# Attention, Fourier mixing and an MLP in one kernel: the first pass of the second product summed over two chunks in PSUM

## The chip, the cores and the metric

The kernel runs on one core of a Trainium2 chip. The metric is the time of one execution on the device in microseconds (us), the median over the runs. Five engines work side by side, each on its own queue in program order: TensorE (PE, with weight loads as PEld), VectorE (DVE), ScalarE (ACT), GpSimd (POOL) and SyncE (SP), which issues the transfers. Matmuls write into PSUM, eight banks per core; everything else lies in SBUF.

## The reference

Inputs are q, k and v of shape (4, 12, 448, 64) and two weight matrices in 64-bit floats, 768 x 3072 and 3072 x 768.

```python
scores = where(causal_mask, -1e9, q @ k.T / sqrt(64))
x = softmax(scores) @ v                      # to (4, 448, 768)
mixed = real(fft(fft(x, axis=1), axis=2))    # along rows, then along columns
u = x + mixed
un = (u - mean(u)) / sqrt(var(u) + 1e-6)
out = u + maximum(un @ w_ch1, 0) @ w_ch2
```

## The kernel before

All products are done with operands split in a high and a low part in the format fp32r: a product is three matmuls, high x high, high x low and low x high, summed in PSUM. Names ending in h and l are these parts.

The program is not written in the order in which it runs. Each step is declared with `add` (an engine or a choice of engines, a cost, a priority, what it reads and writes); `Plan.order` (line 101) then picks step by step the one that can start first by these costs, with the priority to break ties, and chooses between VectorE, ScalarE and GpSimd where a step may run on several. So a changed cost, priority or buffer count can move instructions on all engines, in stages that the change does not name too. The constants at the top (lines 30 to 51) set priorities and buffers.

The stages are: attention (`attend`) for 24 pairs of heads; `fold` and `dft`, the Fourier transform as products with cosine and sine tables, then the normalization; then the MLP. The MLP goes over the 1792 rows in two passes ("groups" g = 0 and 1, two batches or 896 rows each) and in each pass over 12 chunks of 256 hidden columns (`items`, line 708). For a chunk j:

- `weights` (line 723) loads a half (128 x 768) of w1 or w2 as 64-bit numbers, 32-bit words in pairs, and makes 32-bit floats of them with integer and float operations on the words: two on ScalarE (lines 742 and 746), three on VectorE (lines 752, 758 and 762). In the first pass there are 48 such halves. The buffers are w (raw) and w32 (result), two each. For w2 a ScalarE cast makes the high part w2h (line 775) and GpSimd the low part w2l (line 779); there are four buffers of each. Results are also stored to DRAM for the second pass. `halves` splits w1 into its parts (w1, with sums in ws, lines 811 and 824).
- `f1` (line 987) makes the first product into PSUM banks "h". Up to chunk 4 of the first pass, four blocks of the result take eight block products of nine matmuls each (448 columns). From chunk C_FAST = 5 on, and in the whole second pass, `fast` holds: the four blocks are made by seven block products, with sums and differences of the operands (names t1 to t4, s1 to s4). In these, a bank is gone on with after its content has been copied out ("c", line 335 on ScalarE) or added to a copy (line 1051 on VectorE). `finish` writes relu(h) as hh (ScalarE, line 1009) and hl (VectorE, line 1015). There are two buffers of hh and of hl. `kept` chunks leave their w1 parts in DRAM for the second pass.
- `f2` (line 1159) makes the second product. In the first pass, for each of seven blocks of 128 rows and two halves of the 768 columns, six matmuls of 384 columns (two halves of the chunk, three parts) go to a bank "o2" (line 1219), and VectorE adds it to the accumulator "acc" in SBUF (line 1168). That is 14 additions per chunk. In the second pass (`twice`) it is done in seven products again (line 1180).

Around it, `prep`, `mixed` and `refill` make the operands u and t of a pass. The loop at the end (from line 1251) declares for each j the weights ahead of time, then f1 of chunk j + 1 and f2 of chunk j: the first product of the next chunk runs between the matmuls of the second product of this one.

## Time and profile before

| | before |
|---|---|
| median of 3 runs | 944.24 us (944.07 to 949.7) |
| span of the profiled execution | 942.7 us (its own time isn't listed) |
| TensorE busy | 903.4 us, 96% of the span, 5636 matmuls |
| VectorE busy | 796.9 us, 85%, 1330 instructions |
| GpSimd busy | 627.6 us, 67%, 648 |
| ScalarE busy | 545.3 us, 58%, 1300 |
| moved by DMA | 165.84 MB, mean 176 GB/s |

The span runs from the first to the last instruction of the profiled execution; the times of the runs hold a little more. Shares of busy time are means over stages with different limits, so the sections below read them by stage. Matmuls overlap, and the end of one is modelled, so a matmul's duration is about twice the distance at which the next one starts; the distance between starts is what a matmul costs. In the timeline a row gives its start, its duration, and in brackets how long the engine idled before it and for what.

### The profile page before, as it was taken

The numbers are of one execution on the slowest core, as the hardware profiler recorded it, in microseconds if no ns is written. First come the engines' busy times: TensorE is split into PE (matmuls) and PEld (weight loads), VectorE is DVE, ScalarE is ACT, GpSimd is POOL, SyncE is SP. The second block draws the span as 40 slices with busy tenths as digits, with TensorE's granted clock in tenths as the row PEclk, the third lists the DMA queues.
The fourth block names the chain that finished last, engine by engine and source line by source line (L and its number), as shares of the span: only waits on it lengthen the run. The fifth ranks groups of instructions, "written<-read, shape, count | busy, mean of one in ns | idle before, by whom it ended". The sixth has DMA issues, their size and how long they took to land.

```text
span 942.7 us, 16159 instructions
## 1 busy us (share of the span) xinstructions
PE 903.4 (96%) x5636; PEld 805.8 (85%) x5636; DVE 796.9 (85%) x1330; ACT 545.3 (58%) x1300; POOL 627.6 (67%) x648
## 2 busy tenths in 40 slices
PE   7999999999799999999999988999999999999998
PEld 4667668777688999988989887998999999999998
DVE  6889999898897887999998999997788676666668
ACT  6999798988644444545454456645454453444442
POOL 4798698884642222443543337799999898887886
PEclk9999999999899999999999999999999999999999
DMA  7624624615569556758777668665123444444403
GB/s 274 220 88 170 183 77 138 164 45 180 149 210 345 171 208 224 245 196 292 277 275 256 214 217 295 210 217 174 48 68 118 129 139 136 141 145 136 149 1 117
DMA packets 67537, 165.84 MB, mean 176 GB/s; under 512 B 18976, under 2 KB 31904, under 8 KB 67360
## 3 DMA queue, kind: packets, MB, share of 16 engines
q1 hardware_dynamic: 67456, 164.82, 52.8%
q8 instruction: 44, 0.72, 0.3%
q14 instruction: 37, 0.30, 0.1%
HBM read 112.89 MB, written 54.74 MB: 178 GB/s over the span
## 4 chain that ended last, share of the span: by engine, by line
PE 60%; DVE 21%; POOL 6%; issue 6%; ACT 6%; DMA 1%; SPq 0%; POOLq 0%; DVEq 0%; ACTq 0%
PE h L978 22%; PE o L1180 16%; PE o L1219 8%; PE x L531 4%; PE pt L505 3%; PE sc L457 3%; DVE acc L1168 3%; DVE w L762 3%; DVE w L752 2%; ACT p L473 2%; DVE w L811 1%; DVE w L758 1%; DVE mn L469 1%; DVE ws L824 1%; DVE hl L1015 1%
## 5 line engine op out<-in xcount | busy, mean ns | idle before, releaser
L1168 DVE TENSOR_TENSOR acc<-o,acc 128x384 f32<-128x384 f32 x444 | 236.8, 552 | 79.9 <-PE o L1180 56.3
L1219 PE MATMUL o<-w2l,hh 128*128 128x384 f32 x336 | 113.6, 338 | 1.4 <-POOL w2l L779 1.3
L1219 PE MATMUL o<-w2h,hh 128*128 128x384 f32 x336 | 113.3, 337 | 1.6 <-DVE acc L1168 1.6
L1219 PE MATMUL o<-w2h,hl 128*128 128x384 f32 x336 | 113.1, 337 | 0.0
L779 POOL TENSOR_TENSOR w2l<-w,w2h 128x768 fp32r<-128x768 f32 x24 | 49.7, 2071 | 78.6 <-ACT w2h L775 71.6
L494 POOL TENSOR_TENSOR p<-p,ri 128x128 f32<-128x128 f32 (+3 forms) x113 | 79.1, 729 | 22.0 <-DVE ri L485 18.1
L811 POOL TENSOR_TENSOR w<-w,w 128x384 fp32r<-128x384 f32 x33 | 39.7, 1203 | 60.1 <-ACT w L335 59.1
L978 PE MATMUL h<-u11h,w 128*128 128x448 f32 x174 | 64.8, 380 | 3.4 <-ACT u11h L335 3.0
L1219 PEld LDWEIGHTS o<-w2l,hh 128*128 128x128 f32 x336 | 63.1, 188 | 4.4 <-POOL w2l L779 2.6
L1219 PEld LDWEIGHTS o<-w2h,hh 128*128 128x128 f32 x336 | 63.2, 188 | 4.2 <-DVE acc L1168 2.3
L978 PE MATMUL h<-u22h,w 128*128 128x448 f32 x174 | 63.2, 371 | 3.2 <-DVE c L1051 3.2
L1180 PE MATMUL o<-w2h,hh 128*128 128x384 f32 x288 | 65.1, 339 | 0.3 <-DVE acc L1168 0.3
L978 PE MATMUL h<-u12h,w 128*128 128x448 f32 x174 | 64.1, 370 | 0.0
L1219 PEld LDWEIGHTS o<-w2h,hl 128*128 128x128 f32 x336 | 63.2, 188 | 0.0
L978 PE MATMUL h<-u21h,w 128*128 128x448 f32 x174 | 63.0, 367 | 0.0
L1180 PE MATMUL o<-w2l,hl 128*128 128x384 f32 x288 | 62.4, 338 | 0.4 <-DVE acc L1168 0.4
L505 PE MATMUL pt<-cst,p 128*128 128x128 f32 (+1 forms) x384 | 56.9, 281 | 2.6 <-ACT p L492 1.9
L505 PEld LDWEIGHTS pt<-cst,p 128*128 128x128 f32 (+1 forms) x384 | 41.4, 139 | 16.8 <-issue 5.7
L335 ACT COPY c<-h 128x448 f32<-128x448 f32 x57 | 30.1, 529 | 44.1 <-PE h L978 40.2
L867 POOL TENSOR_TENSOR w2h<-w,w2h 128x384 fp32r<-128x384 f32 x43 | 45.8, 1065 | 14.6 <-ACT w2h L335 14.6
L473 ACT ACTIVATE p<-sc,mn 128x448 f32<-128x448 f32 (+3 forms) x96 | 50.4, 525 | 7.6 <-DVE mn L469 6.7
L1180 PEld LDWEIGHTS o<-w2h,hh 128*128 128x128 f32 x288 | 52.1, 188 | 2.6 <-DVE acc L1168 0.6
(212 smaller groups left out, 2999.7 us busy)
## 6 DMA issues: line engine op xcount, KB each, us to landing
w<-in_w_dram SPq DMA_DIRECT2D x48, 768.0 KB, 4.9
wp<-w SPq DMA_DIRECT2D x49, 384.0 KB, 3.5
w<-wp SPq DMA_DIRECT2D x49, 384.0 KB, 3.1
wf<-w SPq DMA_DIRECT2D x34, 384.0 KB, 2.9
w<-wf SPq DMA_DIRECT2D x17, 768.0 KB, 4.3
raw<-in_qk_dram SPq DMA_DIRECT2D x23, 480.0 KB, 3.8
us<-und SPq DMA_DIRECT2D x45, 224.0 KB, 4.2
v<-in_vv_dram SPq DMA_DIRECT2D x24, 256.0 KB, 2.9
```

Of the source, the lines that this page charges most:

```text
L335: nc.scalar.copy(out=out, in_=in_)
L473: nc.scalar.activation(out=T[pb][:, PO[rr]:PO[rr] + n], in_=T[ps][:, c0:c0 + n], func=ACTF.Exp, scale=-1.0, bias=T[mn][:, rr:rr + 1], accu ...
L494: nc.gpsimd.tensor_tensor(out=x, in0=x, in1=z.to_broadcast([128, KE[r]]), op=ALU.mult)
L505: nc.tensor.transpose(T[ps][0:m, 128 * k:128 * k + 128], T[pb][:, PO[r] + 128 * c:PO[r] + 128 * c + m], T["cst", 0][:, 0:128])
L531: nc.tensor.matmul(out=T[xps][64 * h:64 * h + 64, q0:q0 + w], lhsT=T[v][0:kk, c, h * D:(h + 1) * D], rhs=T[src][0:kk, s0 + h * sd:s0 + h * ...
L779: nc.gpsimd.tensor_tensor(out=T[wl], in0=T[w32].bitcast(F32), in1=T[wh], op=ALU.subtract)
L811: (nc.gpsimd if eng == "G" else nc.vector).tensor_tensor(out=T[z][:, 1], in0=src(), in1=T[z][:, 0], op=ALU.subtract)
L867: (nc.gpsimd if eng == "G" else nc.vector).tensor_tensor(out=T[z][:, 384:768], in0=src(), in1=T[z][:, 0:384], op=ALU.subtract)
L978: nc.tensor.matmul(out=T[ps][:, 0:S], lhsT=a[:, t], rhs=x[:, t], start=start and k == 0, stop=stop and k == 8, skip_group_check=True)
L1168: nc.vector.tensor_tensor(out=x, in0=T[ps][:, 0:384], in1=x, op=ALU.add)
L1180: nc.tensor.matmul(out=T[ps][:, 0:384], lhsT=hpart(j, h, a)[:, k * 128:k * 128 + 128], rhs=T[z][:, 384 * b:384 * b + 384], start=start and ...
L1219: nc.tensor.matmul(out=T[ps][:, 0:384], lhsT=T[a][:, m, k * 128:(k + 1) * 128], rhs=w[:, sl], start=(m == 0 and z == 0), stop=(m == 1 and ...
```

## The change

In the first pass the second product is made for two chunks at once: f2 runs for odd j only and sums the four halves of chunks j - 1 and j, twelve matmuls into a bank, before VectorE adds it to the accumulator. The accumulators are loaded at chunk 1 instead of 0. The declarations of a pair change with it: f1 of both chunks of the next pair follows f2 of this one (`f1_at`, `ahead`), the weights are declared in the order of their priorities (`jobs`), and a set of constants gives the places.

In the conversion of weights a third ScalarE operation puts the sign into the top byte of the low word, and the VectorE operation that took it from the high word (line 752) is dropped; the scale goes from the minimum on VectorE (line 758) to ScalarE's absolute value.

The raw and converted weights get three and four buffers instead of two and two, w1 eight instead of seven; the room is taken from the scratch for DMA descriptors, set to 1024 bytes. C_FAST goes from 5 to 4, so chunk 4 of the first pass is done in seven products too. SLOW and LATER, with which the planner chooses between engines, and the places MIX_LEAD and FILL_LEAD change.

```diff
-N_RAW, N_V, N_QK, N_PT, N_W, N_W32, N_PA = 2, 2, 3, 2, 2, 2, 2
+N_RAW, N_V, N_QK, N_PT, N_W, N_W32, N_PA = 2, 2, 3, 2, 3, 4, 2
-W_LEAD, F2_LAG = 809, 561
+W_LEAD, F2_LAG = 362, 453
+PAIR_F1, PAIR_GAP, PAIR_LEAD, F2_PAIR, PAIR_STEP, PAIR_W = 967, 652, 1010, 100, 67, 140
-N_W1, N_C, N_WS, C_FAST, C_MIX = 7, 3, 3, 5, 7
-MIX_LEAD, FILL_LEAD = -94, 417
-LATER = dict(S=-1500, V=-248, G=-847)
+N_W1, N_C, N_WS, C_FAST, C_MIX, N_W2 = 8, 3, 3, 4, 8, 4
+MIX_LEAD, FILL_LEAD = -372, 141
+LATER = dict(S=-1500, V=-599, G=-787)
-SLOW, BIAS = 1.5, dict(S=-300, V=-100, G=-500)
+SLOW, BIAS = 1.639, dict(S=-300, V=-100, G=-500)
...
-            nc.scalar.activation(out=T[w32].bitcast(F32), in_=T[w][:, :, 1].bitcast(F32), func=ACTF.Abs)
+            nc.scalar.activation(out=T[w32].bitcast(F32), in_=T[w][:, :, 1].bitcast(F32), func=ACTF.Abs, scale=W_SCALE)
...
-            x = T[w][:, :, 1]
-            nc.vector.scalar_tensor_tensor(
-                out=x, in0=x, scalar=0x80000000, in1=T[w][:, :, 0], op0=ALU.bitwise_and, op1=ALU.bitwise_or)
+            nc.scalar.activation(
+                out=T[w].bitcast(I8)[:, :, 3], in_=T[w][:, :, 1].bitcast(F32), func=ACTF.Prelu, scale=SIGN_SCALE, alpha=SIGN_ALPHA)
...
-            nc.vector.tensor_scalar(out=x, in0=x, scalar1=W_HIGH, scalar2=W_SCALE, op0=ALU.min, op1=ALU.mult)
+            nc.vector.tensor_scalar(out=x, in0=x, scalar1=W_TOP, scalar2=None, op0=ALU.min)
...
-                out=T[w32], in0=T[w32], scalar=3, in1=T[w][:, :, 1], op0=ALU.logical_shift_left, op1=ALU.bitwise_or)
+                out=T[w32], in0=T[w32], scalar=3, in1=T[w][:, :, 0], op0=ALU.logical_shift_left, op1=ALU.bitwise_or)
...
-        hh, hl = ("hh", j), ("hl", j)
+        js = (j - 1, j)
...
-                    for m in range(2):
-                        wh, wl = T["w2h", (j, m)], T["w2l", (j, m)]
+                    for q, (y, m) in enumerate((y, m) for y in js for m in range(2)):
+                        hh, hl, wh, wl = T["hh", y], T["hl", y], T["w2h", (y, m)], T["w2l", (y, m)]
...
-                                start=(m == 0 and z == 0), stop=(m == 1 and z == 2))
+                                start=(q == 0 and z == 0), stop=(q == 3 and z == 2))
...
-            f1(j + 1, when(j))
-        f2(j, when(j) + F2_LAG, 1000 / 14)
+        elif j % 2:
+            f2(j, when(j - 1) + F2_PAIR, PAIR_STEP)
+            for k in ((j + 1, j + 2) if j + 1 < NCH else (j + 1,)):
+                ahead(k)
...
-    nc = _bacc.Bacc("TRN2", target_bir_lowering=False, num_devices=1)
+    nc = _bacc.Bacc("TRN2", target_bir_lowering=False, num_devices=1, dynamic_dma_scratch_size=1024)
```

What the planner makes of it stands in two places. The first is TensorE's queue in the middle of the second product of the first pass, with matmuls as out<-moving operand, weights; o2 is a bank of the second product, h one of the first. Before:

```order
L1219 MATMUL o2_6333<-w2h_6153,hh_5885 128x384
L1219 MATMUL o2_6333<-w2l_6164,hh_5885 128x384
L1219 MATMUL o2_6333<-w2h_6153,hl_5897 128x384
L978 MATMUL h_6322<-u21h_3954,w1_6284 128x448
L978 MATMUL h_6322<-u21l_3978,w1_6284 128x448
L978 MATMUL h_6322<-u21h_3954,w1_6284 128x448
L1219 MATMUL o2_6351<-w2h_6123,hh_5885 128x384
L1219 MATMUL o2_6351<-w2l_6128,hh_5885 128x384
L1219 MATMUL o2_6351<-w2h_6123,hl_5897 128x384
L1219 MATMUL o2_6351<-w2h_6153,hh_5885 128x384
L1219 MATMUL o2_6351<-w2l_6164,hh_5885 128x384
L1219 MATMUL o2_6351<-w2h_6153,hl_5897 128x384
```

And now, one bank:

```order
L1221 MATMUL o2_6913<-w2h_6497,hh_6526 128x384
L1221 MATMUL o2_6913<-w2l_6508,hh_6526 128x384
L1221 MATMUL o2_6913<-w2h_6497,hl_6538 128x384
L1221 MATMUL o2_6913<-w2h_6503,hh_6526 128x384
L1221 MATMUL o2_6913<-w2l_6521,hh_6526 128x384
L1221 MATMUL o2_6913<-w2h_6503,hl_6538 128x384
L1221 MATMUL o2_6913<-w2h_6570,hh_6682 128x384
L1221 MATMUL o2_6913<-w2l_6582,hh_6682 128x384
L1221 MATMUL o2_6913<-w2h_6570,hl_6692 128x384
L1221 MATMUL o2_6913<-w2h_6646,hh_6682 128x384
L1221 MATMUL o2_6913<-w2l_6657,hh_6682 128x384
L1221 MATMUL o2_6913<-w2h_6646,hl_6692 128x384
```

Before, six matmuls made a bank and first products stood between the banks. Now twelve make one, from two hidden tiles and four halves of w2, and the 14 banks of a pair follow one another, with at most three first-product matmuls among them: 168 matmuls, then a block of 105 to 150 first-product matmuls, and so on through the pass.

The second place is TensorE's queue inside the first product of a chunk done in seven products, where bank h changes from the operand t3 to t4. Before:

```order
L978 MATMUL h_6280<-t3l_4512,w1_6358 128x448
L978 MATMUL h_6280<-t3h_4508,w1_6358 128x448 x2
L978 MATMUL h_6280<-t3l_4512,w1_6358 128x448
L978 MATMUL h_6280<-t3h_4508,w1_6358 128x448
L978 MATMUL h_6280<-t4h_5402,w1_6361 128x448
L978 MATMUL h_6280<-t4l_5413,w1_6361 128x448
L978 MATMUL h_6280<-t4h_5402,w1_6361 128x448 x2
L978 MATMUL h_6280<-t4l_5413,w1_6361 128x448
```

And now:

```order
L980 MATMUL h_7079<-t3h_4462,w1_7091 128x448 x2
L980 MATMUL h_7079<-t3l_4475,w1_7091 128x448
L980 MATMUL h_7079<-t3h_4462,w1_7091 128x448
L980 MATMUL h_7249<-u11h_7159,w1_7208 128x448
L980 MATMUL h_7249<-u11l_7240,w1_7208 128x448
L980 MATMUL h_7249<-u11h_7159,w1_7208 128x448
L980 MATMUL h_7256<-u21h_7173,w1_7212 128x448
L980 MATMUL h_7256<-u21l_7188,w1_7212 128x448
L980 MATMUL h_7256<-u21h_7173,w1_7212 128x448
L980 MATMUL h_7079<-t4h_5114,w1_7133 128x448
L980 MATMUL h_7079<-t4l_5138,w1_7133 128x448
L980 MATMUL h_7079<-t4h_5114,w1_7133 128x448
```

Before, t4 followed t3 in the same bank with nothing between them. Now six matmuls into two other banks, of the next chunk, stand there.

## Rows read from the trace of the kernel before

**Rows 1.** The page's head: the span.

```profile
span 942.7 us, 16159 instructions
```

**Rows 2.** Busy time by stretch: stretch, its length, PE, PEld, DVE, ACT, POOL, PEclk, DMA.

```profile
0.00:241.50 241.50, 227.44 (x2042) 165.41 (x2042) 208.64 (x432) 209.98 (x650) 183.95 (x240) 1.00 0.49 155
241.50:292.60 51.10, 46.48 (x273) 42.80 (x274) 46.81 (x69) 25.30 (x47) 26.68 (x26) 0.93 0.67 204
292.60:645.30 352.70, 336.62 (x1766) 317.20 (x1765) 318.52 (x457) 177.67 (x297) 161.50 (x118) 1.00 0.70 242
645.30:939.20 293.90, 292.83 (x1559) 280.40 (x1557) 222.35 (x373) 132.37 (x308) 255.46 (x267) 1.00 0.34 109
...
300.00:380.00 80.00, 80.00 (x428) 76.53 (x427) 64.58 (x104) 38.39 (x58) 18.46 (x13) 1.00 0.61 213
380.00:640.00 260.00, 244.91 (x1286) 229.87 (x1285) 245.45 (x344) 133.30 (x230) 136.39 (x99) 1.00 0.71 246
```

**Rows 3.** TensorE's timeline, 331 to 342 us: start, duration, what.

```profile
331.47 0.34 PE L1219 MATMUL o<-w2h,hh 128*128 128x384 f32 x1
...
332.52 0.36 PE L978 MATMUL h<-u11h,w 128*128 128x448 f32 x1
...
333.13 0.34 PE L1219 MATMUL o<-w2h,hh 128*128 128x384 f32 x1
...
336.45 0.37 PE L978 MATMUL h<-u12h,w 128*128 128x448 f32 x1
...
339.55 0.34 PE L1219 MATMUL o<-w2h,hh 128*128 128x384 f32 x1
...
341.64 0.37 PE L978 MATMUL h<-u22h,w 128*128 128x448 f32 x1
```

**Rows 4.** TensorE's timeline where it idled; in brackets the idling and its releaser.

```profile
294.71 0.45 PE L1219 MATMUL o<-w2l,hh 128*128 128x384 f32 x1 [0.99 <-POOL w2l L779]
...
552.90 0.47 PE L978 MATMUL h<-t4h,w 128*128 128x448 f32 x1 [0.62 <-ACT c L335]
...
556.75 0.47 PE L978 MATMUL h<-u22h,w 128*128 128x448 f32 x1 [1.75 <-DVE c L1051]
...
585.80 0.48 PE L978 MATMUL h<-t4h,w 128*128 128x448 f32 x1 [2.78 <-ACT c L335]
...
639.84 0.74 PE L978 MATMUL h<-t2h,w 128*128 128x448 f32 x1 [2.33 <-ACT c L335]
640.38 0.58 PE L978 MATMUL h<-t2l,w 128*128 128x448 f32 x1
640.75 0.58 PE L978 MATMUL h<-t2h,w 128*128 128x448 f32 x1
```

**Rows 5.** Groups by form: busy us, mean ns of one, idle us before them.

```profile
L1168 DVE TENSOR_TENSOR acc<-o,acc 128x384 f32<-128x384 f32 x444 | 236.8, 552 | 79.9 <-PE o L1180 56.3 <-PE o L1219 20.6
...
L762 DVE SCALAR_TENSOR_TENSOR w<-w,w 128x768 uint32<-128x768 uint32 x48 | 54.1, 1128 | 0.2
...
L752 DVE SCALAR_TENSOR_TENSOR w<-w 128x768 uint32<-128x768 uint32 x48 | 52.0, 1083 | 1.4 <-ACT w L742 1.0 <-ACT w L746 0.2
...
L746 ACT ACTIVATE w<-w 128x768 uint32<-128x768 uint8 x48 | 43.8, 913 | 12.9 <-DMA w<-in_w_dram 10.4 <-DVE t2l L905 2.5
...
L758 DVE TENSOR_SCALAR w<-w 128x768 f32<-128x768 f32 x48 | 34.4, 719 | 0.6 <-ACT w L742 0.6
...
L335 ACT COPY c<-h 128x448 f32<-128x448 f32 x57 | 30.1, 529 | 44.1 <-PE h L978 40.2 <-POOL us L1118 3.6
```

**Rows 6.** One line each: durations in ns, min/median/max, first and last start.

```profile
L752 DVE SCALAR_TENSOR_TENSOR w<-w x48: 909/953/2260, 119.8 to 610.9; 128x768 uint32<-128x768 uint32 x48
...
L758 DVE TENSOR_SCALAR w<-w x48: 507/551/1514, 132.7 to 610.4; 128x768 f32<-128x768 f32 x48
...
L762 DVE SCALAR_TENSOR_TENSOR w<-w,w x48: 941/949/2586, 137.7 to 612.2; 128x768 uint32<-128x768 uint32 x48
...
L775 ACT CAST w2h<-w x24: 820/834/840, 290.1 to 613.7; 128x768 fp32r<-128x768 f32 x24
...
L779 POOL TENSOR_TENSOR w2l<-w,w2h x24: 1837/1858/3950, 291.0 to 615.6; 128x768 fp32r<-128x768 f32 x24
```

More of the change, by code (lines that the diff above doesn't have):

```diff
@@ L14 @@
 U8 = mybir.dt.uint8
+I8 = mybir.dt.int8
 ACTF = mybir.ActivationFunctionType
@@ L1249, in w1s, with f1_at, go, ahead @@
         halves(j, p0 + 10)
+    def f1_at(j):
+        if items[j][0]:
+            return when(j - 1), 1.0
+        if j < 2:
+            return when(-1) + PAIR_GAP * j, 0.5
+        return when(j - j % 2 - 2) + PAIR_F1 + PAIR_GAP * (j % 2), 0.5
     prep(0, when(-1) - 300)
[L1252 removed]
+    jobs = []
     for j in range(J):
[L1254 to L1257 removed]
+        p = f1_at(j)[0] - W_LEAD if j else when(-1) - 300
+        jobs.append((p, len(jobs), lambda j=j, p=p: w1s(j, p)))
         if twice(j):
[L1259 to L1270 removed]
+            def go(j=j, p=when(j) - W_LEAD + 750):
+                weights(j, "2", 1, p)
+                quarters(j, p)
+            jobs.append((when(j) - W_LEAD + 750, len(jobs), go))
+        else:
+            for half in range(2):
+                p = when(j - j % 2) + F2_PAIR - PAIR_LEAD + PAIR_W * (2 * (j % 2) + half)
+                jobs.append((p, len(jobs), lambda j=j, p=p, half=half: weights(j, "2", half, p)))
+    for _, _, go in sorted(jobs, key=lambda x: x[:2]):
+        go()
+    def ahead(j):
+        if items[j] == (0, C_FAST):
+            mixed(0, f1_at(j)[0] - MIX_LEAD, False)
+        if items[j] == (0, C_MIX):
+            mixed(1, f1_at(j)[0] + 500, True)
+        if items[j] == (1, 0):
+            refill(1, f1_at(j)[0] - FILL_LEAD)
+        f1(j, *f1_at(j))
+    ahead(0)
+    ahead(1)
+    for j in range(J):
+        if twice(j):
+            if j + 1 < J:
+                ahead(j + 1)
+            f2(j, when(j) + F2_LAG, 1000 / 14)
+        elif j % 2:
+            f2(j, when(j - 1) + F2_PAIR, PAIR_STEP)
+            for k in ((j + 1, j + 2) if j + 1 < NCH else (j + 1,)):
+                ahead(k)
     seq = plan.order()
```

41 lines of the change are left out of this document (14 added, 27 removed).

## The prediction

> **What bounds the kernel now.** I began with the span and then cut it into stages by the busy time of each engine [rows 1, 2]. The reader is to see four stages: attention and Fourier transform (0 to 241.5 us), a crossover (241.5 to 292.6), the first pass of the MLP (292.6 to 645.3) and the second pass (645.3 to 939.2). TensorE is busy for 91% or more of each (227.44 of 241.5, 46.48 of 51.1), so it sets the end, and what a change elsewhere is worth is only the time in which TensorE stands still for it. That time is not spread evenly. The second pass has 292.83 us busy of 293.90; the first pass has 336.62 of 352.70, so 16.1 us of visible idling. Inside the first pass it sits in one part: from 300 to 380 us TensorE is busy for 80.00 of 80.00 us, with VectorE at 64.58 (81%) and GpSimd at 18.46 (23%); from 380 to 640 us it is 244.91 of 260, with VectorE at 245.45 (94%) and GpSimd at 136.39 (52%) [rows 2].
>
> A busy TensorE still hides small gaps, so I also counted. In the timeline six matmuls of the second product (384 columns) start within 1.05 us, 0.175 each, and three of the first (448 columns) within 0.61 us, 0.2033 each [rows 3]. The first pass holds 12 x 84 = 1008 of the former, and by the order of the program 756 of the latter (1764 together; the window counts 1766). That is 176.4 + 153.7 = 330.1 us of work in 352.7: 22.6 us are lost there, and this is what the change can win.
>
> Where they are lost the waits say [rows 4]. From chunk 5 on the first product is done in seven products instead of eight, which share a bank: before "t4" may go on in it, ScalarE must have copied out what "t3" left (a copy of 0.529 us [rows 5]). TensorE idles there for 0.62 us at the least and 2.78 at the most (five such rows before 640 us, 6.0 us), and 1.75 at "u22", which waits for VectorE's addition (three rows, 3.2 us). VectorE is late since its queue is full, and what fills it can be read off its groups: the additions to the accumulators (444 x 0.552 us) and three operations per half of weights in the conversion, 48 x 1.128, 48 x 1.083, 48 x 0.719 [rows 5].
>
> **The change part by part.** *Sum of two chunks in PSUM.* In the first pass 168 additions become 84: 84 x 0.552 = 46.4 us less on VectorE. The matmuls stay.
>
> *Conversion.* VectorE loses 48 x 1.083 = 52.0 us. ScalarE gains 48 instructions; no row has that function with an 8-bit result, the nearest (an 8-bit source, same 768 elements) takes 0.913, so 43.8 us. Bounds: 0.529 (the shortest row of that size class) and twice 0.913; I take 0.913. ScalarE is busy 177.67 of 352.7 us in the first pass, so there is room on average; its in-order queue is a rival below. The order has one table load in either program, so the new function brings none.
>
> *What moves.* VectorE goes from 1328 to 1247 instructions, not by 132 but by 81: 51 come over or are new, most of them from GpSimd (628 to 600). At the 0.719 to 1.128 of its two-operand and long rows I price them at 0.88, 45 us. VectorE in the first pass: 318.5 - 46.4 - 42 x 1.083 (six halves are converted before it) + 45 = 272 us of some 338, 80%: the load at which TensorE lost nothing visible between 300 and 380 us.
>
> *The order on TensorE.* Before, nothing stands between "t3" and "t4"; now six matmuls of other banks do, 1.2 us, more than the 0.529 us copy, and "t4" and "u22" come in threes by turns. So most of the 9.2 us in those eight rows should go.
>
> *What is late next.* A sum over two chunks needs both hidden tiles and four halves of w2, and there are just two hidden and four w2 buffers: nothing of the next pair can be written until the last matmul of this pair has read. Before, the first such start waited 0.99 us for GpSimd's w2l [rows 4]. I allow 1 us for each of six pairs, and 0.4 us for each of eight seven-product chunks: 9 us lost in place of 22.6, so 13.6 gained. Bounds: 0 lost (300 to 380 us) and 22.6.
>
> *One more chunk in seven products* (chunk 4): nine matmuls less, 9 x 0.2033 = 1.8 us. Its extra additions fall on VectorE (three, 1.8 us) under the cover above.
>
> *Long blocks.* First-product matmuls alone start 0.2067 us apart (15 in 3.10), not 0.2033; second-product ones alone 0.1742 (12 in 2.09), not 0.175 [rows 3]. 663 x 0.0034 - 1008 x 0.0008 = 1.4 us lost.
>
> *Attention and crossover.* Two more halves are converted during attention and the constants shift a few operations; ScalarE is busy 209.98 of 241.5 there. Two halves are six ScalarE and four VectorE instructions, some 9 us beside TensorE's 227: from 4 us lost to 3 gained, I take 0. In the crossover VectorE is busy for 46.81 of 51.1 us [rows 2] and loses an operation per half: 1 us gained, bounds 0 and 3. The smaller scratch for DMA descriptors only frees room: in the order every transfer stands in SyncE's queue and none in GpSimd's; taken at 0 (bounds -1 and +1).
>
> **Sum** against the profiled execution: 942.7 - 13.6 - 1.8 + 1.4 - 1 = 927.7 us of span. That execution's own time is not listed; the median 944.24 stands 1.5 us above its span, so 929 us.
>
> One rule speaks to the size of this. VectorE's conversion steps have medians of 0.953, 0.551 and 0.949 us but reach 2.26, 1.51 and 2.59, and GpSimd's w2l goes from 1.84 to 3.95 [rows 6]. The Trainium skill, page "SBUF — State Buffer", section "SBUF: two separate sides", says VectorE and GpSimd take their common port pair as an exclusive lock, so that the second waits for the whole instruction of the first. The long maxima agree with that. By it a first pass with less on GpSimd gets its medians back, 42 x (0.168 + 0.179) = 14.6 us less on VectorE, 76% busy, the load of the second pass, and I would put the loss at 5 us and the time at 925. I stay with the means.
>
> **Rivals.** *Nothing gained (0.16).* The 51 instructions fill VectorE again and the copies stay late: 22.6 us lost as before, and only 1.8 - 1.4 gained: 944. For it: the program was balanced by moving work over. Against: the six matmuls between "t3" and "t4" don't depend on VectorE's load.
>
> *ScalarE becomes the late one (0.10).* Each half now puts three instructions of 0.91 us on ScalarE, and a copy that TensorE waits for stands behind one of them. Eight chunks with three copies each, at half an instruction, 24 x 0.46 = 11 us: 940. For it: the row with 2.78 us. Against: ScalarE had half its time free.
>
> *The pair starts late, slower than before (0.11).* Between two pairs' sums TensorE has only the first products of two chunks, 105, 117, 138, 147 and 150 matmuls by the order, 21.3 to 30.5 us. In that time four halves of w2 must go through ScalarE, VectorE twice, ScalarE and GpSimd. Wholly in series at these rows' medians a half takes 0.913 + 0.551 + 0.949 + 0.834 + 1.858 = 5.1 us, four 20.4; at the maxima 9.8 and 39.2. If it takes 33 us, the five blocks are overrun by 11.7 + 9.2 + 4.9 + 3.1 + 2.5 = 31 us, less the 5 allowed: 955, and after such gaps the clock falls too (after 2.33 us of idling matmuls started 0.37 us apart instead of 0.2033 [rows 4], the level of 1.2 GHz): 957. It decides from about 32 us on. Against: two of the four halves are converted before the block starts.
>
> *Everything hidden (0.03):* no loss in the first pass, 920.
>
> *The forecast (0.60):* 929, its own range 920 to 938.
>
> **How the numbers follow.** A measurement of this kernel can tell about 1% from no change. Faster by more (under 934.8): the forecast but for its upper tail, and the hidden case, 0.64. Within 1%: nothing gained, ScalarE late, a little of the forecast, 0.25. Slower (over 953.7): 0.11. The range goes from 917 (all hidden and 3 us at the crossover) to 946, which takes in "nothing gained" with 2 us lost in attention; outside are the late pair and a little below.
>
> **What would show it.** Right: the addition to the accumulators at 360 instructions; VectorE at 78 to 83% of the first pass; TensorE's visible idling there at 5 to 8 us instead of 16, "t4" no longer a row with over 1 us; first pass 337 to 341 us long, the second within 2 us of 293.9, the start of the first second-product matmul within 3 us of 292.6. Wrong: waits of TensorE for w2l over 2 us at the start of a pair (then the late pair), waits for c copies behind weight conversions (then ScalarE), VectorE above 90% (then nothing gained), or a shift before 292.6 us, which I put at 0 or 1.

## The result and the profile after

The changed kernel takes 958.32 us (median of 4 runs, 955.77 to 960.02) against 944.79 us before: a ratio of 1.0126, interval 1.0094 to 1.0158. It is slower by 1.3%, where 1.6% faster was forecast, and lies above the range. The profiled execution took 957.12 us with a span of 955.3 us, 12.6 us over the span of before [rows 1].

A row product is a block product of the MLP's first product, into the banks "h". Busy time by stretch, cut where the first row product starts, where the first second product starts (the first pass) and where the last second product of that pass ends, answers to [rows 2]: stretch, length, PE, PEld, DVE, ACT, POOL with instruction counts, granted clock, DMA share, GB/s.

```profile
0.00:248.70 248.70, 233.76 (x2043) 170.11 (x2043) 213.06 (x448) 218.15 (x651) 180.93 (x238) 0.98 0.50 160
248.70:301.45 52.75, 48.82 (x275) 43.56 (x274) 42.75 (x66) 31.22 (x52) 23.18 (x25) 0.88 0.69 225
301.45:641.20 339.75, 322.51 (x1674) 302.53 (x1673) 244.63 (x368) 228.06 (x302) 95.33 (x61) 0.98 0.69 242
641.20:951.80 310.60, 309.28 (x1641) 296.23 (x1639) 219.64 (x374) 141.50 (x327) 273.23 (x288) 1.00 0.34 114
```

VectorE did what was forecast: in the first pass it is busy 244.63 of 339.75 us, 72%, where it was 90%. TensorE got nothing for it. With the distances between matmuls of the prediction (1008 x 0.175, and 663 row matmuls by the timeline x 0.2033) the first pass holds 311.2 us of work in 339.5: 28.3 us are lost, where 22.6 were. I use this "loss" for every run below. The 12.6 us are then:

| | before | after | |
|---|---|---|---|
| start of the first row product | 241.5 | 248.7 | +7.2 |
| crossover | 51.2 | 52.8 | +1.5 |
| loss of the first pass | 22.6 | 28.3 | +5.7 |
| nine row matmuls fewer (chunk 4) | | | -1.8 |

The first pass is 13 us shorter and the second 17 us longer: 84 row matmuls (17.1 us) moved from one to the other, as they now stand behind the last second product of the first pass. The second pass loses no more than before.

What TensorE waits for, from the view of waits (operation, releaser: us in total, times, longest). Before:

```profile
PE h L978 <- ACT c L335: 9.3, 7, 2.8
PE at L695 <- DVE un L685: 3.8, 4, 2.0
PE h L978 <- DVE c L1051: 3.2, 3, 1.7
PE h L978 <- ACT u11h L335: 3.0, 1, 3.0
PE h L978 <- DVE u11l L905: 2.6, 1, 2.6
...
PE h L978 <- DVE w L811: 0.4, 1, 0.4
```

After:

```profile
PE at L698 <- DVE un L688: 8.0, 5, 4.2
PE h L980 <- ACT w L338: 3.7, 3, 1.5
PE h L980 <- ACT c L338: 3.4, 7, 1.2
PE h L980 <- DVE w L813: 3.1, 4, 1.7
PE h L980 <- DVE u21l L907: 2.5, 1, 2.5
PE h L980 <- DVE c L1053: 2.0, 3, 1.3
PE o L1221 <- POOL w2l L781: 1.7, 2, 1.3
```

The wait for the copies "c" fell from 9.3 to 3.4 us, as forecast. In its place stand waits for parts of w1 (3.7 for ScalarE's high parts, 3.1 for VectorE's low parts, 0.4 before). Around the first row product the waits only change their name: "un" has 8.0 us for 3.8 (4.18 of it right before that product), and the parts of "u" have 2.7 (2.49 and 0.23) for 5.6. In the timeline, beside [rows 4]:

```profile
247.66 1.35 PE L698 MATMUL at<-cst,un 112*128 112x112 f32 x6 [4.18 <-DVE un L688]
...
255.99 0.74 PE L980 MATMUL h<-u21l,w 128*128 128x448 f32 x1 [2.49 <-DVE u21l L907]
...
419.56 0.47 PE L980 MATMUL h<-u11h,w 128*128 128x448 f32 x1 [1.46 <-ACT w L338]
...
528.30 0.48 PE L980 MATMUL h<-t4h,w 128*128 128x448 f32 x1 [0.43 <-ACT c L338]
537.98 0.47 PE L980 MATMUL h<-u11h,w 128*128 128x448 f32 x1 [1.41 <-ACT w L338]
...
602.53 0.74 PE L980 MATMUL h<-u21h,w 128*128 128x448 f32 x1 [0.77 <-DVE w L813]
```

"t4" no longer waits over 0.5 us; a new chunk's "u11" and "u21", which need a part of w1 just made, do. Neither belongs to the sums over pairs alone. Two runs below, e6 and e14, sum over pairs with the old conversion, and in the first pass they wait for w1 parts 0 and 0.7 us and for the copies again 8.3 and 9.7 (e6, then e14):

```profile
PE h L981 <- ACT c L338: 8.3, 5, 4.0
...
PE h L981 <- ACT c L338: 9.7, 10, 2.2
```

Groups, beside [rows 5]:

```profile
L1170 DVE TENSOR_TENSOR acc<-o,acc 128x384 f32<-128x384 f32 x360 | 195.7, 555 | 111.2 <-PE o L1182 58.0 <-PE o L1221 51.8
...
L754 ACT ACTIVATE w<-w 128x768 int8<-128x768 f32 x48 | 94.0, 1959 | 0.9
...
L764 DVE SCALAR_TENSOR_TENSOR w<-w,w 128x768 uint32<-128x768 uint32 x48 | 51.7, 1078 | 19.4 <-ACT w L754 19.1
...
L749 ACT ACTIVATE w<-w 128x768 uint32<-128x768 uint8 x48 | 44.3, 922 | 0.1
```

The additions went from 444 to 360 as the change says. ScalarE's new step takes 1959 ns, not the 913 of its neighbour, and VectorE's last conversion step now idles 19.1 us for it.

Some of what the waits cost comes after them, through TensorE's clock. Around the end of attention, in stretches of 4 us of after (columns as above):

```profile
244.00:248.00 4.00, 0.34 (x2) 0.37 (x3) 3.56 (x4) 2.10 (x5) 3.10 (x3) 0.94 1.05 289
248.00:252.00 4.00, 3.77 (x13) 2.63 (x11) 3.87 (x5) 3.42 (x7) 3.42 (x4) 0.50 0.78 278
252.00:256.00 4.00, 1.51 (x5) 0.84 (x4) 2.94 (x3) 2.40 (x2) 4.00 (x5) 0.50 0.84 259
256.00:260.00 4.00, 4.00 (x11) 3.57 (x12) 4.00 (x5) 1.87 (x3) 0.79 (x1) 0.50 0.24 73
260.00:264.00 4.00, 4.00 (x33) 3.84 (x32) 1.72 (x4) 1.25 (x3) 1.65 (x1) 0.85 0.91 272
```

TensorE stands still for most of 4 us, and then runs at half its clock, 1.2 GHz, until past 260 us, 11 matmuls in its fully busy 4 us. Before, the same place looks like this:

```profile
240.00:244.00 4.00, 0.47 (x1) 0.19 (x1) 3.68 (x4) 4.00 (x9) 4.00 (x3) 0.94 0.19 56
244.00:248.00 4.00, 3.42 (x9) 3.11 (x10) 4.00 (x5) 2.14 (x5) 3.48 (x4) 0.50 0.60 164
248.00:252.00 4.00, 4.00 (x15) 3.60 (x15) 4.00 (x6) 0.35 (x2) 3.39 (x3) 0.70 0.64 189
252.00:256.00 4.00, 4.00 (x22) 3.63 (x21) 3.72 (x4) 3.23 (x7) 1.59 (x1) 1.00 0.29 94
```

Here the clock is back by 252 us, with 22 matmuls in the last 4 us. In after a second wait (2.49 us, up to 255.99) falls into the slow stretch, which by these rows lasts 13.7 us where it lasted 6.9. Over all stretches of 8 us, busy time of TensorE times what the clock lacks of 1 comes to 4.1 us before (2.3 of it in the crossover) and 13.6 us after: 4.0 in attention, 5.4 in the crossover, 4.2 in the first pass (after the waits at 305 and 602 us). So 9.5 us more of clock are given up in after. That is time of TensorE, not all of it reaches the end, and it is no separate cause. The larger part of attention's share comes long before the first weights are converted (88.9 us):

```profile
12.00:16.00 4.00, 3.74 (x22) 2.71 (x24) 2.92 (x9) 1.78 (x5) 1.29 (x2) 0.50 0.71 236
16.00:20.00 4.00, 4.00 (x29) 2.78 (x28) 2.40 (x6) 3.54 (x14) 3.50 (x6) 0.64 0.97 318
```

Before, in the same stretches:

```profile
12.00:16.00 4.00, 3.86 (x36) 2.72 (x38) 3.06 (x10) 2.52 (x10) 2.46 (x5) 1.00 0.77 245
16.00:20.00 4.00, 3.27 (x28) 2.35 (x28) 3.55 (x11) 3.96 (x16) 3.29 (x6) 1.00 0.99 357
```

The clock didn't fall here, though TensorE waits alike just ahead of it (1.43 and 0.67 us; in after 1.43 and 0.66). And nothing of these 3.3 us (3.74 x 0.50 + 4.00 x 0.36) is left later: by 145 us both kernels have 1194 and 1193 matmuls behind them. The 7.2 us of the later start arise after that. The Trainium skill, page "TensorE: Matmul & The Clock Gate", section "HAM oscillation — how this bites in real kernels", says that waits between groups of matmuls send the array back to the low clock and that this is paid at each of them; the rows around the end of attention agree, though the 2.78 us in [rows 4] brought no fall, and the same waits near 12 us brought one in after and none before.

### The profile page after: what moved, and what is told of

It is laid out like the page before. It is cut to its first block, busy times and chain, and to the rows that moved or that the text cites. A ratio compares the mean times of both kernels' runs of the same rounds, so it can differ in the third digit from the quotient of the medians.

```text
span 955.3 us, 16028 instructions
## 1 busy us (share of the span) xinstructions
PE 914.4 (96%) x5627; PEld 812.4 (85%) x5627; DVE 720.6 (75%) x1252; ACT 618.9 (65%) x1331; POOL 572.7 (60%) x609
## 5 line engine op out<-in xcount | busy, mean ns | idle before, releaser
L1170 DVE TENSOR_TENSOR acc<-o,acc 128x384 f32<-128x384 f32 x360 | 195.7, 555 | 111.2 <-PE o L1182 58.0
L754 ACT ACTIVATE w<-w 128x768 int8<-128x768 f32 x48 | 94.0, 1959 | 0.9
L497 POOL TENSOR_TENSOR p<-p,ri 128x128 f32<-128x128 f32 (+3 forms) x109 | 75.0, 717 | 22.8 <-DVE ri L488 14.9
L826 POOL TENSOR_TENSOR ws<-w,w 128x384 f32<-128x384 f32 x8 | 9.8, 1220 | 126.3 <-DVE w L764 126.3
L764 DVE SCALAR_TENSOR_TENSOR w<-w,w 128x768 uint32<-128x768 uint32 x48 | 51.7, 1078 | 19.4 <-ACT w L754 19.1
L1221 PEld LDWEIGHTS o<-w2h,hh 128*128 128x128 f32 x336 | 63.7, 190 | 0.1
L980 PE MATMUL h<-u12h,w 128*128 128x448 f32 x168 | 61.0, 368 | 0.0
L476 ACT ACTIVATE p<-sc,mn 128x448 f32<-128x448 f32 (+3 forms) x96 | 50.9, 531 | 11.2 <-DVE mn L472 9.7
```

Source lines behind the costliest of these rows:

```text
L476: nc.scalar.activation(out=T[pb][:, PO[rr]:PO[rr] + n], in_=T[ps][:, c0:c0 + n], func=ACTF.Exp, scale=-1.0, bias=T[mn][:, rr:rr + 1], accu ...
L497: nc.gpsimd.tensor_tensor(out=x, in0=x, in1=z.to_broadcast([128, KE[r]]), op=ALU.mult)
L754: nc.scalar.activation(out=T[w].bitcast(I8)[:, :, 3], in_=T[w][:, :, 1].bitcast(F32), func=ACTF.Prelu, scale=SIGN_SCALE, alpha=SIGN_ALPHA)
L764: nc.vector.scalar_tensor_tensor(out=T[w32], in0=T[w32], scalar=3, in1=T[w][:, :, 0], op0=ALU.logical_shift_left, op1=ALU.bitwise_or)
L980: nc.tensor.matmul(out=T[ps][:, 0:S], lhsT=a[:, t], rhs=x[:, t], start=start and k == 0, stop=stop and k == 8, skip_group_check=True)
L1170: nc.vector.tensor_tensor(out=x, in0=T[ps][:, 0:384], in1=x, op=ALU.add)
```

## The experiments

Times are medians; each ratio is to the kernel before on the same chip, with its 95% interval. "Start" is that of the first row product, "loss" that of the first pass, "second" the loss of the second pass (its length less 900 x 0.175 and its row matmuls x 0.2033). These three are of the profiled execution; in e5 and e6 that was the slowest and the fastest of ten, 4.8 us above and 4.0 below the median. "Leads" are the planner's constants for priorities and for choosing engines. Where they are "own", they were chosen anew for that kernel, by the planner's own schedule and without the chip. "7" means chunk 4 in seven products; "larger" are the buffers of the change for raw and converted weights, w1 keeping seven where sums are of one chunk.

| run | second product | conversion (planner's cost) | buffers, leads | us | ratio | start | loss | second |
|---|---|---|---|---|---|---|---|---|
| before | chunk | old | two | 944.79 | 1 | 241.5 | 22.6 | 2.5 |
| after | pair | new (0.81) | larger, 7 | 958.32 | 1.0126 [1.0094, 1.0158] | 248.7 | 28.3 | 2.7 |
| e1_copy8 | pair | Copy to int8 | as after | 957.32 | 1.0121 [1.0068, 1.0175] | 248.0 | 25.0 | 5.8 |
| e2_prelu16 | pair | to 16 bits | as after | 960.96 | 1.0153 [1.0110, 1.0196] | 250.0 | 30.0 | 7.4 |
| e5_word32 | pair | to 32 bits | as after | 952.10 | 1.0059 [1.0035, 1.0084] | 245.5 | 20.5 | 12.9 |
| e3_conv_only | chunk | new (0.81) | as before | 955.07 | 1.0088 [1.0061, 1.0114] | 247.2 | 31.0 | 2.7 |
| e4_pairs_only | pair | old | as after | 959.67 | 1.0140 [1.0099, 1.0182] | 241.0 | 36.7 | 7.3 |
| e6_pairs_tuned | pair | old | larger, own, 7 | 948.29 | 1.0024 [0.9991, 1.0057] | 243.7 | 19.6 | 1.0 |
| e14_pairs_again | pair | old | larger, own, 7 | 954.15 | 1.0097 [1.0061, 1.0134] | 248.7 | 15.0 | 11.2 |
| e7_cost_tuned | pair | new (1.95) | larger, own, 7 | 944.30 | 0.9979 [0.9957, 1.0001] | 250.6 | 18.4 | 2.5 |
| e11_cost_again | pair | new (1.95) | larger, own, 7 | 946.51 | 1.0006 [0.9983, 1.0030] | 247.5 | 16.6 | 8.4 |
| e10_old_cost | pair | new (0.81) | larger, own, 7 | 949.26 | 1.0036 [1.0007, 1.0065] | 253.2 | 19.8 | 1.5 |
| e12_old_again | pair | new (0.81) | larger, own, 7 | 956.99 | 1.0121 [1.0084, 1.0158] | 250.9 | 25.1 | 7.7 |
| e8_buffers_only | chunk | old | larger, as before | 947.54 | 0.9997 [0.9964, 1.0029] | 250.8 | 15.5 | 8.4 |
| e16_leads_only | chunk | old | two, own | 953.51 | 1.0081 [1.0052, 1.0111] | 241.6 | 12.4 | 18.2 |
| e9_buffers_tuned | chunk | old | larger, own, 7 | 934.18 | 0.9882 [0.9828, 0.9936] | 245.5 | 14.8 | 1.2 |
| e15_buffers_again | chunk | old | larger, own, 7 | 930.64 | 0.9839 [0.9811, 0.9868] | 247.9 | 7.9 | 3.3 |
| e13_single_new | chunk | new (1.95) | larger, own, 7 | 930.61 | 0.9836 [0.9806, 0.9865] | 251.3 | 3.1 | 2.0 |
| e17_blocks | chunk, in blocks | old | as e15 | 942.66 | 0.9955 [0.9933, 0.9977] | 246.6 | 20.3 | 4.2 |
| e18_blocks_new | chunk, in blocks | new (1.95) | as e13 | 947.28 | 1.0011 [0.9980, 1.0043] | 261.2 | 6.9 | 5.0 |

**The new ScalarE step.** Two theories first: the step is slow and holds ScalarE's queue (S), or sums over pairs lose by themselves (P). What makes it slow, the function or the narrow result? (e1 and e5 leave out the sign of the weights; orders are those of after.)

```diff
-out=T[w].bitcast(I8)[:, :, 3], in_=T[w][:, :, 1].bitcast(F32), func=ACTF.Prelu, scale=SIGN_SCALE, alpha=SIGN_ALPHA)
+out=T[w].bitcast(I8)[:, :, 3], in_=T[w][:, :, 1].bitcast(F32), func=ACTF.Copy, scale=SIGN_SCALE)                       # e1
+out=T[w].bitcast(I16)[:, :, 1], in_=T[w][:, :, 1].bitcast(F32), func=ACTF.Prelu, scale=SIGN_SCALE, alpha=SIGN_ALPHA)    # e2
+out=T[w][:, :, 1].bitcast(F32), in_=T[w][:, :, 1].bitcast(F32), func=ACTF.Prelu, scale=SIGN_SCALE, alpha=SIGN_ALPHA)    # e5
```

> The changed kernel with Copy instead of Prelu in the new ScalarE step, still written as 8-bit numbers; the order on all engines stays as it is. The sign of the weights is lost, so the output is not the reference's. Theory S (the new step takes 1.96 us instead of the 0.91 I priced, 48 times, and holds up ScalarE's queue): if Copy brings it to about 0.91, the first first-product matmul comes back from 248.7 to 242 to 244 us, the first pass from 340 to 325 to 330 us, the whole to 938 to 944 us. Theory P (what costs is the sum over pairs itself, without spare hidden and w2 buffers): the whole stays at 953 to 957 us though the step is shorter. If the step stays at 1.95 us, the 8-bit result is what is slow, and the time stays at 955 to 960.

> The changed kernel with the Prelu written as 16-bit numbers into the upper half of the low word (the sign is then in the same place). If the 8-bit result is what makes the step slow, it falls to about 0.91 us and theory S expects 938 to 944 us, theory P 953 to 957. If Prelu itself is slow, the step stays at 1.95 us and the time at 955 to 960.

> The changed kernel with one edit: ScalarE's new step writes its 768 results as 32-bit words into the words it read, where nothing reads them, so the weights lose their sign (that part of the conversion is left out); order, buffers and planner's costs stay. If the 1.96 us of the new step are what costs (theory S), the step falls to about 0.91 us (as the other step that writes 32-bit words eight bytes apart, 0.911), the first row product starts at 241 to 243 us again and the time is 928 to 942 us. If the sums over pairs lose by themselves (theory P, as the run with the old conversion, which lost 36.7 us in the first pass), the start comes back but the first pass still loses 25 us or more and the time is 948 to 955. If the width of the result isn't what slows the step, it stays at 1.96 us and the time at 957.

The step's row in e1_copy8 (durations in ns: min/median/max; first and last start; shapes):

```profile
L754 ACT ACTIVATE w<-w x48: 1917/1953/2020, 88.5 to 582.3; 128x768 int8<-128x768 f32 x48
```

and in e5_word32:

```profile
L754 ACT ACTIVATE w<-w x48: 882/906/967, 88.2 to 576.8; 128x768 f32<-128x768 f32 x48
```

Another function takes as long, 16 bits take as long (a mean of 1960 ns), a 32-bit result at the same step of eight bytes takes 0.906 us. So the narrow result makes the step slow. In e5_word32, same order, the start comes 3.2 us earlier, the loss is 7.8 us lower, and the waits for w1 parts are 3.9 us instead of 6.8. But theory S had expected 942 us or less, and 952.1 came; P's time came, its loss of 25 us or more did not. The medians of after and e5 lie 6.2 us apart, and that is what the slow step is seen to cost. (Its profiled execution, the slowest of ten, gave 10.2 us back in the second pass, where additions to "acc" came late; why, and whether the signless values have a part in it, is open.)

**One part at a time.** e3_conv_only is before with the new conversion alone; e4_pairs_only is after with the old one, by taking this part of the change out again:

```diff
-            nc.scalar.activation(
-                out=T[w].bitcast(I8)[:, :, 3], in_=T[w][:, :, 1].bitcast(F32), func=ACTF.Prelu, scale=SIGN_SCALE, alpha=SIGN_ALPHA)
+            x = T[w][:, :, 1]
+            nc.vector.scalar_tensor_tensor(
+                out=x, in0=x, scalar=0x80000000, in1=T[w][:, :, 0], op0=ALU.bitwise_and, op1=ALU.bitwise_or)
```

> The kernel before with the new conversion alone (three steps on ScalarE, two on VectorE), with the buffers, constants and chunk by chunk sums of before. Theory S: VectorE has 52 us less, ScalarE 94 us more, and the attention stage and the handing over of banks wait for ScalarE: 948 to 955 us, first first-product matmul 3 to 6 us later than 241.5. Theory P: the conversion is a gain by itself, 934 to 942 us.

> The changed kernel with the old conversion (two steps on ScalarE, three on VectorE), all else as changed. Theory S: the sums over pairs are a gain when ScalarE is not held up: 930 to 940 us, first pass 322 to 332 us. Theory P: 950 to 960 us, with TensorE's idling in the first pass still above 16 us.

Each part alone is slower than before, and together they are no worse than each: the losses don't add. In these two the start moves with the conversion (247.2 with it, 241.0 without). In e4 TensorE waits 9.8 us in the first pass for w2 (6.1 for w2l, 3.7 for w2h): the late pair of the prediction. Both runs kept leads that were made for another kernel, so they tell the worth of neither part; a third theory came up here, that the planner's orders are wrong for what the step really takes (C).

**The planner's cost.** e7 and e11 count the step at 1.95 us, with two sets of leads; e10 and e12 keep 0.81 with two sets.

```diff
-        add("S", acts(768) + 75, p0 + 1, f, rd=[w, (*w, 1)], wr=[(*w, 2)], phase="W")
+        add("S", acts(768) + 1220, p0 + 1, f, rd=[w, (*w, 1)], wr=[(*w, 2)], phase="W")    # e7, e11
-W_LEAD, F2_LAG = 362, 453
+W_LEAD, F2_LAG = 362, 337      # e7; PAIR_F1 753, PAIR_GAP 842, F2_PAIR 287, FILL_LEAD -130, V -728, G -589
+W_LEAD, F2_LAG = 362, 631      # e11; PAIR_LEAD 989, PAIR_W 150, C_MIX 7, FILL_LEAD -216, V -672
```

> The changed kernel with the planner's cost of the new ScalarE step at 1.95 us in place of 0.81, and its leads and lags chosen anew for that cost. If the wrong cost in the planner (theory C) is what loses, the time is 938 to 946 us. If the step's length itself is what loses (theory S: 48 x 1.05 us more of ScalarE's in-order queue in attention and the first pass), it stays at 950 us or more.

> The changed kernel with its cost of 0.81 us for the new ScalarE step left in the planner, and only the leads and lags chosen anew (W_LEAD 321, F2_LAG 334, PAIR_F1 950, PAIR_LEAD 1024, FILL_LEAD 1097, LATER, SLOW). Theory C (the wrong cost is what loses): 953 us or more, as after. Theory N (any new order of the same work lands somewhere in a band of some 15 us, by which waits of TensorE come together and drop its clock): anywhere from 942 to 957, and under 950 would refute C.

> The changed kernel with the cost of 1.95 us in the planner, and a second, other set of leads and lags. Theory C: 941 to 949 us, as with the first set (944.3). Theory N: anywhere from 942 to 957; 952 or more would refute C.

> As the run with the cost of 0.81 us kept, with a second, other set of leads and lags (W_LEAD 275, F2_LAG 350, PAIR_F1 991, C_MIX 7, SLOW 1.334). Theory C: 953 us or more. Theory N: anywhere from 942 to 957, and the mean granted clock tells where: 0.982 or less goes with 952 or more, 0.987 or more with 946 or less.

With the true cost 944.3 and 946.5 us, no different from before; with the wrong one 949.3 and 957.0, and 958.3 in the change itself. C's direction holds in all four, but by the bound set for e10 (under 950) C is refuted as it was stated, and the intervals of e10 and e11, run on the same chip, overlap. The order's luck (N) has a share: the planner's own schedules of e10 and e12 (`Plan.end`) end at 907.1 and 907.8 us, and the chip runs them 8 us apart. In these runs the mean granted clock goes along (0.982 in e12 and after, 0.987 to 0.989 in e7, e10 and e11, 0.991 before); beyond them it doesn't, with 0.990 in e14 at 954 us and 0.987 in e13 at 931.

**Pairs with leads of their own.** e6 and e14 are e4 with two sets.

```diff
-W_LEAD, F2_LAG = 362, 453
+W_LEAD, F2_LAG = 221, 333      # e6; PAIR_F1 775, PAIR_GAP 564, PAIR_LEAD 756, F2_PAIR 186
+W_LEAD, F2_LAG = 229, 1119     # e14; PAIR_F1 298, F2_PAIR 1109, PAIR_STEP -229, SLOW 1.883
```

> Sums over pairs with the old conversion, as in the earlier run of the pairs alone (959.7 us), but with the planner's leads and lags chosen anew for the old conversion (that run kept those of the new one). Theory P (pairs lose whatever the order, for want of a third buffer of hidden rows): first pass still loses 30 us or more, 953 to 960 us. Theory O (the earlier run's loss came from constants that belonged to another conversion): first pass loses 15 to 22 us, 938 to 948 us.

> Sums over pairs, larger buffers, old conversion, with a second set of leads and lags (the first gave 948.3 us). Theory P (the sums over pairs are what costs, since the same without pairs took 934.2): 943 us or more. If order alone decides (theory N): anywhere from 930 to 955, and under 938 would refute P.

The loss fell from 36.7 to 19.6 and 15.0, so e4's leads were indeed wrong; neither time came below before. What e14 takes longer than e6 isn't in the first pass: in the profiled executions, 9.2 us apart, its start is 5.0 us later and its second pass loses 10.2 us more, while its first pass loses less.

**Buffers and leads without pairs.**

```diff
-N_RAW, N_V, N_QK, N_PT, N_W, N_W32, N_PA = 2, 2, 3, 2, 2, 2, 2
+N_RAW, N_V, N_QK, N_PT, N_W, N_W32, N_PA = 2, 2, 3, 2, 3, 4, 2     # e8, e9, e15, with the smaller scratch
-W_LEAD, F2_LAG = 809, 561
+W_LEAD, F2_LAG = 793, 394      # e9; C_FAST 4, C_MIX 6, MIX_LEAD 72, V -140, G -540, SLOW 1.857
+W_LEAD, F2_LAG = 809, 359      # e15; C_FAST 4, C_MIX 9, MIX_LEAD 95, V -784, G -1150, SLOW 1.733
+W_LEAD, F2_LAG = 791, 1049     # e16, two buffers; C_FAST 6, C_MIX 9, FILL_LEAD 217
```

> The kernel before with only the third part of the change: three buffers of raw weights for two, four of converted ones for two, and the DMA scratch made smaller to pay for them; sums of one chunk and the old conversion stay. If the buffers were worth nothing (as the prediction had it), 943 to 946 us. If weights that are converted earlier remove waits of the first pass, 930 to 940. If earlier conversion crowds VectorE in attention, 948 or more.

> The kernel before with the larger weight buffers alone (947.5 us before, with the leads of two buffers) and the planner's leads and lags chosen anew for them, chunk 4 in seven products too. Theory B (the buffers are the useful part of the change, but the earlier run converted weights inside attention and so began its first row product 9 us late): first product at 240 to 245 us, first pass loses 12 to 17 us, 928 to 938 us. If attention pays whenever weights are converted earlier: 943 to 948 us.

> Sums of one chunk, larger buffers, old conversion, chunk 4 in seven products, with a second set of leads and lags (the first gave 934.2 us). Theory B (buffers and leads that fit them are worth some 10 us): 930 to 939 us. Theory N: anywhere from 930 to 950, and 943 or more would refute B.

> The kernel before with its two buffers of raw and two of converted weights, and only the leads and lags chosen anew (chunk 4 and 5 in eight products). If the gain of the larger buffers came from new leads alone: 930 to 939 us. Theory B (it takes the buffers): 941 to 947 us.

Buffers alone changed nothing in the time: the loss of the first pass fell by 7 us, that of the crossover by 5, the start came 9 us later and the second pass lost 6 us more. New leads alone lost 0.8%, outside both of the ranges expected for e16. Both together, with chunk 4 in seven products, gained 1.2% and 1.6%. But e16's first pass, with two buffers, lost ten us less than before and no more than e9's; what made it slow is its second pass, with these waits:

```profile
PE o L1180 <- DVE acc L1168: 5.3, 6, 2.2
PE h L978 <- DVE w L811: 4.1, 1, 4.1
```

So buffers and leads together, which I priced at nothing, can be made to pay; that it takes the buffers isn't shown.

**The new conversion without pairs.** e13 is e15's kernel with the new conversion at 1.95 us and W_LEAD 802, F2_LAG 420, MIX_LEAD -94, FILL_LEAD -561, C_MIX 6, SLOW 1.588.

> Sums of one chunk as before, the larger buffers, chunk 4 in seven products, and the new conversion with its cost of 1.95 us in the planner and leads chosen anew. Against the same with the old conversion (934.2 us): if the new conversion is worth its ScalarE time once it is planned for (theory A), 925 to 934. If it costs (theory S: the 50 us more of ScalarE come due in attention), 938 to 948 us, with the first row product 3 us or more later than at 245.5.

930.6 us, the fastest of all beside e15 and faster than both kernels of this study. Its first pass:

```profile
310.15:628.70 318.55, 316.58 (x1693) 303.40 (x1692) 273.37 (x424) 231.79 (x318) 151.02 (x111) 1.00 0.76 256
```

TensorE is busy 316.58 of 318.55 us, VectorE 86%: the loss is 3.1 us, less than the 9 that I had forecast for the change. But it starts 3.4 us later than e15, and the times are equal. The conversion moves 3 to 5 us from the first pass into attention; with sums of one chunk, and planned for, it brings nothing that is seen. (With pairs, e7 and e11 against e6 and e14, it is 2 to 10 us, about as much as two sets of leads differ.) S's bound of 938 is refuted, A's holds.

**Why pairs lose.** With the larger buffers and leads of their own, sums of one chunk take 930.6 to 934.2 us (three runs), pairs 944 to 957 (six). The planner's own schedules of these kernels end at 896.1 to 900.1 and 907.1 to 909.6 us (before 913.3, after 910.5), so the planner, which knows no clock, already counts about half of this against the pairs: that half lies in what waits for what. TensorE changes between the two products 212 times in the first pass before, 256 times in e13 and 15 times in after: with two buffers of hidden rows a pair uses both, so no second product is left to stand between the block products of the next pair (theory I). In after 14.3 of the 17.2 us of visible idling lie inside stretches of 24 to 38 us with row products alone. To test it without pairs, e17 and e18 force such blocks on e15 and e13 by their due times (F2_BLOCK is -500; w2 is declared as much earlier):

```diff
+        sc = 1.0 if twice(j) else 0.5
...
-        p = [p0 + 143 * i for i in range(9)]
+        p = [p0 + 143 * sc * i for i in range(9)]
...
-        f2(j, when(j) + F2_LAG, 1000 / 14)
+        f2(j, *((when(j) + F2_LAG, 1000 / 14) if twice(j) else (when(j) + F2_BLOCK, 1000 / 28)))
```

> The kernel with sums of one chunk, larger buffers and the old conversion that took 930.6 us, with the first pass's due times set so that TensorE runs each chunk's row products in one piece and then its 14 second products in one piece, instead of taking turns. Sums, buffers, bytes and the work of every engine stay. Theory I (the sums over pairs cost because with two buffers of hidden rows they leave TensorE no second product to put between the block products that wait; in the changed kernel it changes between the two products 15 times in the first pass, before 212 times): the first pass loses 15 to 25 us for 7.9, 938 to 952 us. If taking turns hides nothing and it is the longer sums themselves: 928 to 935 us.

> The same edit on the kernel with sums of one chunk, larger buffers and the new conversion planned at its true cost (930.6 us; its first pass lost 3.1 us). Theory I: the first pass loses 13 to 25 us, 938 to 952 us. If taking turns hides nothing: 928 to 935 us.

The first pass of e15, by stretch:

```profile
300.55:628.40 327.85, 322.12 (x1715) 307.20 (x1714) 316.27 (x481) 168.42 (x287) 131.30 (x90) 1.00 0.74 256
```

and of e17_blocks:

```profile
309.79:628.60 318.81, 306.32 (x1609) 289.62 (x1608) 303.54 (x447) 155.83 (x260) 141.34 (x98) 0.98 0.71 245
```

TensorE in e17's first pass, where it idles longest and at a changed operand, and at the start of e18's:

```profile
397.04 0.47 PE L979 MATMUL h<-u12h,w 128*128 128x448 f32 x1 [3.23 <-ACT u12h L336]
...
434.64 0.47 PE L979 MATMUL h<-u22h,w 128*128 128x448 f32 x1 [2.34 <-DVE c L1053]
...
550.63 0.47 PE L979 MATMUL h<-t4h,w 128*128 128x448 f32 x1 [1.69 <-ACT c L336]
```

```profile
261.17 0.74 PE L980 MATMUL h<-u11h,w 128*128 128x448 f32 x1 [8.09 <-ACT u11h L338]
```

In e17 the idle time of TensorE goes from 5.7 to 12.5 us, the clock from 1.00 to 0.98, the loss from 7.9 to 20.3 and the time up by 12.0 us: the blocks, with 20 changes between the products instead of 281, cost what the loss says. The edit also brings w2 forward and keeps leads that were chosen for e15, and a share of the 12 us may be theirs: e9 and e15, two sets without blocks, lie 3.5 us apart. (The planner's own schedules put e17 and e18 16.0 and 13.5 us behind e15 and e13.) The waits are for parts of "u" and for the copies; those for w1 parts, 6.8 us in after, are 1.5 here. In e18 the time rose by 16.7 us as theory I said, but not where it said: the first pass lost only 3.8 us more (6.9, where 13 was the least expected), 9.9 us came in before it, with a wait of 8.09 us for the first operand, and 3 in the second pass. So blocks are seen to cost in the first pass when VectorE is as full as in e15 (96%); with the conversion's load taken off it (84%), the blocks of single chunks lost little. The pairs of e7 and e11, with the same conversion, lose 17 to 18 us, and not for want of changes between the products: e7 has 55 of them, e18 23. Their blocks are longer (the five longest last 22 to 33 us, those of e18 14 to 25). That this length is what loses there fits, but was not tried alone, nor was a third buffer of hidden rows. What makes pairs lose is therefore argued, not shown.

## Why the prediction was wrong, step by step

- *"84 x 0.552 us less", "three operations become two", VectorE at 80%.* Right, and better: 360 additions of 0.555 us, VectorE 72% busy in the first pass. That a VectorE at 80% or less loses TensorE nothing was the error: after loses 28 us at 72% and e7 18 at 78%, while e15 loses 8 at 96%. The load of an engine didn't say when its results come.
- *"The order on TensorE: six matmuls between t3 and t4".* Right for this kernel: the waits for the copies fell from 9.3 to 3.4 us. But the planner's order does this, not the sum over pairs: e13 and e15, without pairs, have 6 to 12 matmuls there in every chunk, e6 and e14 none in three of eight, and before had 6 to 18 there in three of eight.
- *"What is late next: 1 us for each of six pairs, for w2l; 9 us lost in place of 22.6".* This step failed most. The waits for w2l are small (1.7 us in all), but I looked only at the second product's operands. What is late in after are the row products' own operands: above all parts of w1 where a new block product starts (6.8 us of waits, 0.4 before), with the 1.96 us step in the chain that makes them (3.9 us of these waits in e5, 0 and 0.7 in e6 and e14 with the old conversion). That it shows because no second product is left to run meanwhile fits e17, but isn't shown for the pairs. I had seen that the 14 banks of a pair follow one another, and priced it only by the distance between matmuls (1.4 us). The bound that I took as the worst, 22.6, was exceeded by 5.7.
- *"No row has that function with an 8-bit result; 0.529 to twice 0.913, I take 0.913".* 1.959 us, above the upper end of 1.83. The row to take was none of those: all the rows that I used have 32-bit results. It cost 50 us more of ScalarE, 6 us of them seen in the end (e5_word32). The same error stood in the planner's cost: three orders made with it took 949.3 to 958.3 us, two made with the true one 944.3 and 946.5. How much of these 3 to 14 us is the cost and how much the order's luck is open.
- *"Attention and crossover: from 4 us lost to 3 gained, I take 0".* 7.2 and 1.5 us lost. Six halves instead of four are converted before the first row product, and the two more were priced at nothing. With the old conversion too, the runs with six halves there start late (e8 250.8, e14 248.7) and those with four at 241.5 and 241.6 (before, e16); with five it is 241.0 to 247.9. The new step adds to it: four halves with it start at 247.2 (e3). I had left the granted clock out of this stage too; its share in the time is not known.
- *Scratch and buffers "taken at 0".* As changed, 0 is right (e8: 0.9997). But together with leads of their own, and chunk 4 in seven products, they are worth 11 and 15 us (e9, e15).
- *Chunk 4, 1.8 us.* Not contradicted: nine matmuls fewer.
- *The rule on the port pair* (the Trainium skill, page "SBUF — State Buffer", section "SBUF: two separate sides"). With GpSimd at 28% of the first pass where it was 46%, VectorE's last conversion step has a mean of 1078 ns for 1128, and two thirds of its excess over the median stay (120 ns for 179). In e13, with GpSimd at 47%, the excess is 82. So the medians that I read out of the rule didn't come, and the excess doesn't follow GpSimd's load here. They wouldn't have helped: with VectorE at 72%, below the 76% that I reckoned by the rule, the loss was 28 us, not 5.
- *Rivals.* The one on the other side, "the pair starts late", named the right side and, with 957 us, the time, but that is luck, for its place was wrong: no wait for w2l is over 1.3 us in this kernel (in e4 it does come). "ScalarE becomes the late one" had the mechanism of ScalarE's queue and a time of 940. I gave the two 0.21 together and had them as alternatives, though nothing keeps both from coming. The chance of "faster by more" was also added up wrong: 0.60 and 0.03 make 0.63 at most, not 0.64.

## What to carry to other kernels

Before a sum is made longer to spare an engine, ask what the longer sum takes from the order: work that ran between dependent products may have hidden their waits. A planner that sets an order by costs has to be given the measured duration of a new step before the change is judged; with its leads chosen anew for the true cost, this change came out even, and with the sums left single it gained 1.6%. Let such a planner also say where each part of a change would end: here it put the pairs 7 us or more behind single sums with the same buffers. A part that gives no time by itself (buffers, e8) may pay when the order is made for it. And compare losses in all stages: several of these orders won in the first pass and lost it again in the second.
